# Bringing two weight matrices in transposed: by the load, in place of TensorE and ScalarE

## The chip, the cores and the metric

The kernel runs on one core of a Trainium2 chip. A core has five engines that run their own instruction streams: TensorE (PE in the profile; its weight loads are listed apart as PEld), VectorE (DVE), ScalarE (ACT), GpSimd (POOL) and SyncE (SP). Data comes from HBM and goes back to it through 16 DMA engines, which SP, ACT and POOL feed: each of the three has a queue of its own, and an issuing engine that has to wait before one transfer holds up every transfer behind it in its queue. The metric is the device time of one execution in microseconds (us). Before the change it is 1417.9 us, the median of 3 runs (1413.8 to 1419.28).

## What is computed

The kernel computes one decode step of a conditioned transformer block and its gradients. The forward, cut to what matters here:

```python
# x: [1,1,640]; k_cache, v_cache: [1,32,8192,192]; all bfloat16
q  = (h @ wq).reshape(32 heads, 192)              # h: layer norm of x, scaled and shifted by mod
p  = softmax(q @ k_cache^T * 192**-0.5)           # over 8192 positions, per head
ao = concat(p @ v_cache) @ wo                     # wo: [6144, 640]
x1 = x + ga * ao                                  # h_b: x1's layer norm, scaled and shifted
h2 = gelu(layernorm(h_b) @ w3) @ w4               # w3: [640, 1536], w4: [1536, 640]
out = x1 + gb * (h_b + h2)
```

The outputs are `out` and the gradients of x, k_cache, v_cache, wq, wo, w3, w4, c and w_mod for a given `grad_out`. (A part of the reference with w1 and w2 drops out, because with one position it only ever sees padding.) Two steps of the backward need a weight matrix with its rows and columns exchanged, since they multiply by its transpose:

- `d_n2 = du @ w3^T`, once, in the middle of the kernel;
- `do = (ga * dx1) @ wo^T`, the gradient at the attention's output, 192 numbers for each head, with rows 384t to 384t+383 of wo for the pair of heads t.

K, V and their gradients are by far the largest tensors: 201 MB of K and V are read for the forward, V is read again for the backward, and 201 MB of gradients are written.

## The kernel before, in words

The numbers that matter: D = 640 (ND = 5 blocks of 128), F = 1536 (NF = 12 blocks), 32 heads of DH = 192, 16 pairs of heads (NT; the last is TL = 15), PW = 384 rows of wo for each pair, P = 128 partitions. TensorE contracts over the partitions, so an operand's contracted index must lie along them. wo as it lies in HBM serves the forward; the backward wants it the other way round.

**Order.** The order of the instructions of TensorE, VectorE, ScalarE and SP is written out by hand (`manual_schedule`): an engine runs them in program order, and where one has to wait, all behind it on that engine wait too. Dependencies alone link the engines.

**Three stages.** First comes the forward over heads 0 to 30, half a head's K or V (1.5 MB) at a time, through five K buffers (`KB`) and three V buffers (`VB`). Then comes the middle: the last head, the MLP's forward and backward, down to `dao`, from which all of the attention's backward starts. Last comes the backward, 64 steps `s` of half a head each, heads in descending order, pair TL first. A step multiplies V with `do` (`mul_q`, VectorE), sums the products with TensorE (`tree_q`, L948) and reduces them to `dP` (L316); from these it makes dK (`dk_part`, VectorE, L964), and dV by outer products on TensorE (`dv_groups`, L959) that ScalarE copies out of PSUM (L960). POOL stores dK (L1214) and dV (L1210); SP loads V for step s+4 (L297).

**w3 in the middle.** w3 is loaded as it lies in HBM, in five row blocks (`w3v`), for the forward product `ups` (L767). For the backward, `w3t_gen` (L745 to L751) makes twelve blocks `w3Tv[a]`: five TensorE transposes of 128x128 into PSUM (L749), then one ScalarE copy (L750). The calls `w3t(n)` are spread between other work from L761 to L842. The blocks lie in two `vs` buffers (T0, T1) and in the first part of the K buffer `KC`, each free once the `m_units` that read it are through. The product with them is `dn_ps` (L850). Ahead of it on the chain: twelve VectorE products `d_g` (`dg_part`, L476), one for each row block of w4, the last of which (`load_rows(..., 11, 12)`, L617) is loaded late because its place in KC has to come free; then `du_bf` (L795).

**wo in the backward.** `load_wo(t)` (L213 to L217) brings a pair's 384 rows as [128, 3, 640] into one of two buffers with the tag `wo`; each partition gets 3840 contiguous bytes. `transposed` (L813 to L822) turns it on TensorE, 15 transposes of 128x128 (L821) with two ScalarE copies (L822), into a tile `wT`; `do_t(t, 0)` and `do_t(t, 8)` are its two parts. `do_mm(t)` (L894) multiplies with the turned tile (L901) and ScalarE scales the result into `do` (L904). The natural tile is then used a second time: `g_dwo` (L1076) overwrites it with wo's gradient, and POOL stores it from there (L1081); only then is the buffer free for another `load_wo`. For pair TL, the tile that the forward used is kept and turned, partly at L846 and partly inside the first `layernorm_bwd` (L914). Pair TL-1 is loaded at L911. The other 14 come from `g_ld`.

**The side jobs.** In the backward, work that isn't part of a step is cut into pieces, listed in `jobs` (L1141 on) and run in order by `slot()`, which is called four times a step. The first eight pieces have slots written by hand (`RAMP`); from slot R0 = 24 the others are spread evenly over the slots up to the 236th. `g_do(n)` was three pieces: `do_t`, `do_t`, `do_mm`. `g_ld`, `g_dwo` and the gradients of wq and w_mod (`g_dq`, `g_wm`, which use `transposed` too) are further jobs.

Of the kernel before, what the change touches and what calls it, by code (L numbers as in the profile page):

```python
# [20 lines left out]
def kernel(  # L21
# [186 lines left out]
    def load_w(view3, lo, hi):  # L208
        w = wst.tile([P, ND, CW], BF16, name="w_st", tag="w", bufs=1)
        nc.sync.dma_start(out=w[:, :, 0 : hi - lo], in_=view3[:, :, lo:hi])  # L210
        return w

# [116 lines left out]
    with tc.tile_pool(name="vs", bufs=3) as vsp, tc.tile_pool(name="ft", bufs=2) as ft, \  # L329
# [149 lines left out]
        with tc.manual_schedule(engines=ORDER):  # L479
# [264 lines left out]

            def w3t_gen():  # L745
                for a in range(NF):
                    tp = psR.tile([P, 1024], BF16, name="w3T_ps", tag="dot_ps")
                    for k in range(ND):
                        T_.transpose(out=tp[:, k * P : (k + 1) * P], in_=w3v[k][:, a * P : (a + 1) * P], identity=ident_bf)  # L749
                    A_.copy(out=w3Tv[a], in_=tp[:, 0:D])  # L750
                    yield  # L751

            w3t_it = w3t_gen()

            def w3t(n):
                for _ in range(n):
                    next(w3t_it, None)

            pe.pop(0)()
            pe.pop(0)()  # L760
            w3t(2)  # L761
            next(g2, None)
# [5 lines left out]
            dg_part(2)  # L768
            w3t(2)
            pe = m_units(3, ky[1], vs3, mp)  # L770
# [7 lines left out]
            V_.tensor_tensor(out=e1, in0=e1, in1=u, op=ALU.mult)  # L778
            w3t(1)
            pe.pop(0)()  # L780
            w3t(1)
            pe.pop(0)()
            pe.pop(0)()
            load_rows(flat(KC)[:, JQ * DH : JQ * DH + D], 11, 12)
            w3t(1)
            V_.tensor_scalar(out=w_, in0=w_, scalar1=1.0, scalar2=None, op0=ALU.add)
# [36 lines left out]

            woT = {}

            def do_t(t, x0):
                if x0 == 0:
                    woT[t] = w4b[:, 0 : 3 * D] if t == TL else bst.tile([P, 15 * P], BF16, name="wT", tag="wT")
                w = wo_l[t]
                transposed(x0, lambda a, b: [(0, P, w[:, a, b * P : (b + 1) * P])], 3, woT[t])  # L830

            er_ps = e_rows(TL - 1, psO, "op")
            er_ps2 = e_rows(TL, psO, "op")
            w3t(1)
            e_rows_out(TL - 1, er_ps)
            h2_mm(0, 2)
            w3t(1)
            e_rows_out(TL, er_ps2, w4b[:, F + D : F + D + P])
            h2_mm(2, 4)
            w3t(1)  # L840
            h2_mm(4, ND)
            w3t(1)  # L842
            mt = mp_out(H1 - 1, mp)
            dw4_dve(flat(KX), 0, 0, 2)
            m_add(H1 - 1, mp, mt)
            do_t(TL, 0)  # L846
            dn_ps = psS.tile([P, ND], FP32, name="dn_ps", tag="s")
# [40 lines left out]
    def do_of(h):  # L888
        return do_r[:, (TL - h // 2) % NDR, (h % 2) * DH : (h % 2 + 1) * DH]
# [20 lines left out]

    wo_l[TL - 1] = load_wo(TL - 1)  # L911
    er_l = {0: load_er(0), 1: load_er(1)}

    layernorm_bwd(d_n2, n2, r2, dbo, d_sb, "lb2", lambda: (do_t(TL, 8), dw4_dve(flat(KX), 0, 2, 4)))  # L914
    d_n1 = tcol(ND, "d_n1")
# [89 lines left out]
    def g_do(n):  # L1005
        do_t(TL - n, 0)
        yield
        do_t(TL - n, 8)
        yield
        assert done_s[0] >= 4 * (n - NDR + 1)  # L1010
        do_mm(TL - n)
        done.add(n)
        yield

    def g_ld(n):
        wo_l[TL - n] = load_wo(TL - n)
        yield
# [58 lines left out]
    def g_dwo(n):  # L1076
        t = TL - n
        w = wo_l.pop(t)
# [274 lines left out]
```

## Time and profile before

| what | us |
|---|---|
| median of 3 runs | 1417.9 |
| the profiled execution | 1418.06 |
| its span | 1416.1 |
| PE busy in it | 1190.1 (84%) |
| VectorE busy | 1108.4 (78%) |
| ScalarE busy | 893.9 (63%) |
| bytes moved by DMA | 569.35 MB, mean 402 GB/s |

The span is the time from the first to the last recorded instruction; all times below are counted from its start. The forward ends near 545 us, the middle lasts to about 583 us, and the backward fills the rest. The groups of instructions that the change concerns, as the profile gives them:

```profile
L749 PE MATMUL w3T_ps<-ident_bf,KB x22: 216/218/229, 561.7 to 570.9; 128*128 128x128 bf16 x22
L750 ACT COPY vs<-w3T_ps x8: 692/693/698, 562.2 to 568.2; 128x640 bf16<-128x640 bf16 x8
L750 ACT COPY KB<-w3T_ps x3: 692/699/712, 569.8 to 573.6; 128x640 bf16<-128x640 bf16 x3
L821 PE MATMUL wT_ps<-ident_bf,wo_st x240: 266/314/314, 573.7 to 1157.7; 128*128 128x128 bf16 x120
L822 ACT COPY wT<-wT_ps x82: 905/976/1032, 603.8 to 1347.3; 128x1024 bf16<-128x1024 bf16 x41, 128x896 bf16<-128x896 bf16 x41
```

Each line has the source line, the engine, the operation with output and inputs, the count, the shortest, median and longest duration in ns, and the first and last start in us. Of the 82 copies of L822 into `wT`, 30 belong to wo; the others belong to the gradients of wq and w_mod, which the change leaves as they are.

### The profile page before, as it was taken

How to read it: one execution, taken by the hardware profiler on the slowest of the kernel's cores; microseconds unless marked ns; L12 is line 12 of the kernel's file. 1: busy time of each engine (PE TensorE's matmuls, PEld its weight loads, DVE VectorE, ACT ScalarE, POOL GpSimd, SP SyncE). 2: the span in 40 equal slices, each digit the busy share in tenths (PEclk: the TensorE clock that was granted, in tenths of full speed). 3: DMA queues.
4: the chain of work that ended last, by engine and by line, in shares of the span. 5: the costliest groups of instructions: out<-in, count | busy, mean ns of one | idle time of the engine just before them, and what ended most of it. 6: DMA issues, size and time to landing. Idle time of an engine off the chain costs nothing.

```text
span 1416.1 us, 30395 instructions
## 1 busy us (share of the span) xinstructions
PE 1190.1 (84%) x12697; PEld 748.8 (53%) x12697; DVE 1108.4 (78%) x1418; ACT 893.9 (63%) x1952; POOL 105.3 (7%) x190
## 2 busy tenths in 40 slices
PE   3888989999999999798867997887978787779975
PEld 2777777777777777543323443443434333334431
DVE  4989999999999997886755875676766767768775
ACT  0767777777777776465645665565655565556664
POOL 0000000000000000110100110111110101111110
PEclk9999999999999999755555555565555655555555
DMA  9999999999999997599999999999999999999998
GB/s 375 394 394 416 418 415 418 411 415 414 422 415 419 411 412 274 178 391 428 424 393 420 427 423 424 420 422 422 425 420 421 411 414 410 405 400 392 424 411 355
DMA packets 76247, 569.35 MB, mean 402 GB/s; under 512 B 7342, under 2 KB 25086, under 8 KB 36046
## 3 DMA queue, kind: packets, MB, share of 16 engines
q1 hardware_dynamic: 51210, 342.02, 59.5%
q0 software_dynamic: 24368, 224.87, 38.1%
q8 instruction: 99, 1.62, 0.4%
q10 hardware_dynamic: 532, 0.53, 0.1%
q14 instruction: 38, 0.31, 0.1%
HBM read 340.95 MB, written 226.43 MB: 401 GB/s over the span
## 4 chain that ended last, share of the span: by engine, by line
issue 47%; DVE 22%; DMA 13%; PE 10%; POOL 6%; ACT 1%; SPq 0%; POOLq 0%; DVEq 0%
DVE prod L302 9%; DMA KB<-in_A_k_cache_dram 8%; DVE prod L306 5%; DVE vs L352 3%; PE mp L374 3%; DMA out_dram<-KB 3%; POOL out_dram L1214 2%; POOL out_dram L1210 2%; DMA w_st<-in_A_wq_dram 2%; PE half_ps L312 2%; PE mp L379 2%; DMA KB<-in_A_v_cache_dram 1%; DVE pq L929 1%; POOL out_dram L1054 1%; DVE KB L964 1%
## 5 line engine op out<-in xcount | busy, mean ns | idle before, releaser
L960 ACT CAST KB<-dv_ps 128x768 bf16<-128x768 f32 x512 | 397.4, 803 | 159.7 <-PE dv_ps L959 157.6
L948 PE MATMUL dot_ps<-pq,ident_bf 128*128 128x256 bf16 x1506 | 383.6, 398 | 24.0 <-DVE dP L316 22.0
L964 DVE TENSOR_TENSOR KB<-qs_bc,dS 128x3072 bf16<-128x3072 bf16 x122 | 210.7, 1753 | 129.0 <-DMA out_dram<-KB 117.0
L359 ACT ACTIVATE vs<-VB,Ef 128x192 bf16<-128x192 bf16 x840 | 303.5, 447 | 0.0
L948 PEld LDWEIGHTS <-ident_bf 128*128 128x128 bf16 x1506 | 151.9, 124 | 179.7 <-issue 140.3
L959 PE MATMUL dv_ps<-do_r,er_b 1*128 1x192 bf16 x2048 | 231.2, 338 | 4.5 <-ACT KB L960 3.2
L929 DVE TENSOR_TENSOR pq<-VB,do_r 128x3072 bf16<-128x3072 bf16 x126 | 220.4, 1749 | 15.7 <-PE dot_ps L948 15.7
L302 DVE TENSOR_TENSOR prod<-KB,qs_bc 128x6144 bf16<-128x6144 bf16 x62 | 207.9, 3353 | 26.6 <-DMA KB<-in_A_k_cache_dram 20.3
L374 PE MATMUL mp<-vs,KB 128*128 128x193 bf16 x1968 | 189.9, 249 | 3.7 <-ACT vs L359 2.6
L374 PEld LDWEIGHTS <-KB 128*128 128x128 bf16 x1984 | 171.1, 98 | 13.1 <-DMA KB<-in_A_k_cache_dram 5.3
L822 ACT COPY wT<-wT_ps 128x1024 bf16<-128x1024 bf16 x82 | 79.0, 964 | 122.6 <-PE wT_ps L821 122.2
L959 PEld LDWEIGHTS <-er_b 1*128 1x128 bf16 x2048 | 69.4, 104 | 157.5 <-issue 154.7
L312 PE MATMUL half_ps<-prod,ident_bf 128*128 128x256 bf16 x744 | 95.1, 279 | 44.4 <-DVE prod L306 44.1
L352 DVE TENSOR_TENSOR vs<-VB,E 128x1728 bf16<-128x1728 bf16 x120 | 123.7, 1052 | 0.3 <-ACT vs L359 0.3
L306 DVE TENSOR_TENSOR prod<-prod 128x3072 bf16<-128x3072 bf16 x62 | 108.7, 1754 | 1.0
L312 PEld LDWEIGHTS <-ident_bf 128*128 128x128 bf16 x744 | 72.9, 100 | 62.7 <-issue 53.6
L379 PE MATMUL mp<-vs,KB 128*64 128x193 bf16 x1968 | 105.9, 250 | 0.0
L316 DVE TENSOR_REDUCE dP<-dot_ps 128x32 f32<-128x512 f32 x64 | 44.0, 688 | 66.9 <-PE dot_ps L948 66.6
L379 PEld LDWEIGHTS <-KB 128*64 128x64 bf16 x1984 | 79.4, 109 | 20.0 <-issue 19.9
L339 ACT ACTIVATE E<-S_h,negm 128x256 bf16<-128x256 f32 x31 | 15.8, 508 | 113.9 <-DVE negm L502 111.6
L1214 POOL DMA_DIRECT2D out_dram<-KB x61 | 33.5, 549 | 475.5 <-DVE KB L964 299.8
L388 PE MATMUL op<-vs,ones_bf 128*32 128x193 bf16 x1920 | 62.1, 250 | 0.0
(300 smaller groups left out, 975.3 us busy)
## 6 DMA issues: line engine op xcount, KB each, us to landing
VB<-in_A_v_cache_dram SPq DMA_DIRECT2D x123, 1536.0 KB
out_dram<-KB POOLq DMA_DIRECT2D x123, 1536.0 KB, 16.0
KB<-in_A_k_cache_dram SPq DMA_DIRECT2D x64, 1536.0 KB
wo_st<-in_A_wo_dram SPq DMA_DIRECT2D x31, 480.0 KB
w_st<-in_A_wq_dram SPq DMA_DIRECT2D x12, 960.0 KB
out_dram<-wo_st POOLq DMA_DIRECT2D x16, 480.0 KB, 16.2
out_dram<-w_st POOLq DMA_DIRECT2D x7, 960.0 KB, 15.4
w_st<-in_w_mod_dram SPq DMA_DIRECT2D x6, 960.0 KB
```

Source lines behind the costliest of these rows:

```text
L302: V_.tensor_tensor(out=prod, in0=src, in1=vec[:, None, :].to_broadcast([P, JH, DH]), op=ALU.mult)
L306: V_.tensor_tensor(out=prod[:, :, 0:HW], in0=prod[:, :, 0:HW], in1=prod[:, :, DH - HW : DH], op=ALU.add)
L312: T_.matmul(ps, lhsT=ident_bf, rhs=prod[:, :, k : k + TF], start=(k == 0), stop=(k == w - TF))
L352: V_.tensor_tensor(out=vs[:, 0:n, 0:DH].rearrange("p j (a b) -> p j a b", b=4), in0=v[:, v0 : v0 + n, :].rearrange("p j (a b) -> p j a b", ...
L359: A_.activation(out=vs[:, k, 0:DH], in_=v[:, v0 + k, :], func=ACT.Copy, scale=Ef[:, j0 + k : j0 + k + 1])
L374: T_.matmul(mp[:, 0:MW], lhsT=kb[:, j0 + k, 0:P], rhs=vs[:, k, 0:MW], start=(q == 0 and k == 0), stop=(z and k == JQ - 1), skip_group_chec ...
L379: T_.matmul(mp[p0 : p0 + 64, MO : MO + MW], lhsT=kb[:, j0 + k, P:DH], rhs=vs[:, k, 0:MW], start=False, stop=(z and k >= JQ - 2), skip_grou ...
L929: V_.tensor_tensor(out=pq[:, q], in0=v_l[s][:, q * JQ : (q + 1) * JQ, :], in1=do_of(ht(s)[0])[:, None, :].to_broadcast([P, JQ, DH]), op=AL ...
L948: T_.matmul(ps[:, q * JQ : (q + 1) * JQ, :], lhsT=ident_bf, rhs=pq[:, q, :, k : k + TS], start=(k == 0), stop=(k == w - TS), skip_group_ch ...
L959: T_.matmul(ps[:, b, k * DH : (k + 1) * DH], lhsT=er[p0 : p0 + 1, 2 * m + k, :], rhs=doh[p0 : p0 + 1, :], start=True, stop=True)
L960: A_.copy(out=dV4[:, 2 * q : 2 * q + 2, m * PW : (m + 1) * PW], in_=ps[:, :, 0:PW])
L964: V_.tensor_tensor(out=dK[:, lo:hi, :].rearrange("p j (a b) -> p j a b", b=4), in0=qh.rearrange("p (a b) -> p a b", b=4)[:, None, :, :].to ...
```

## The change

A load may turn its data on the way: with `transpose=True`, a DMA issued by SP takes a matrix [rows, columns] and puts its columns along the partitions. The change uses that for w3 (three loads, of 512 columns each, into the places where the twelve blocks lay) and for the backward's wo (`load_woT`, one load for each pair). The layout of the turned wo differs from before: within a block of 128 columns of wo, the 384 rows now lie in their natural order, so that `do_mm` reads and writes without its rearranged views. The tile has as many bytes as before, and `g_dwo` still uses it as its output buffer. `do_t` and `w3t_gen` are gone, and `g_do` is one piece in place of three. Pair TL's wo, whose natural tile the forward has, is loaded a second time. `load_wo` stays for the forward, and `transposed` for wq and w_mod.

```diff
+    def load_woT(t):
+        w = wst.tile([P, ND * PW], BF16, name="woT", tag="wo")
+        nc.sync.dma_start(out=w.rearrange("p (i d) -> p i d", i=ND), in_=A_wo[t * PW : (t + 1) * PW, :], transpose=True)
+        return w
...
-            def w3t_gen():
-                for a in range(NF):
-                    tp = psR.tile([P, 1024], BF16, name="w3T_ps", tag="dot_ps")
-                    for k in range(ND):
-                        T_.transpose(out=tp[:, k * P : (k + 1) * P], in_=w3v[k][:, a * P : (a + 1) * P], identity=ident_bf)
-                    A_.copy(out=w3Tv[a], in_=tp[:, 0:D])
-                    yield
...
             pe.pop(0)()
             pe.pop(0)()
-            w3t(2)
+            for k, dst in enumerate((T0, T1, flat(KC))):
+                nc.sync.dma_start(out=dst[:, 0 : 4 * D].rearrange("p (a d) -> p a d", a=4), in_=B_w3[:, 4 * k * P : 4 * (k + 1) * P], transpose=True)
+            wo_l[TL] = load_woT(TL)
             next(g2, None)
...
-            def do_t(t, x0):
-                if x0 == 0:
-                    woT[t] = w4b[:, 0 : 3 * D] if t == TL else bst.tile([P, 15 * P], BF16, name="wT", tag="wT")
-                w = wo_l[t]
-                transposed(x0, lambda a, b: [(0, P, w[:, a, b * P : (b + 1) * P])], 3, woT[t])
...
     def do_mm(t, b=None):
-        wT = woT[t]
+        wT = wo_l[t]
...
         for i in range(ND):
-            rhs = wT[:, i * PW : (i + 1) * PW].rearrange("p (c a) -> p c a", c=3)[:, :, 64 * bs[0] : 64 * bs[-1] + 64]
-            T_.matmul(ps[:, 0:w], lhsT=dao_bf[:, i : i + 1].to_broadcast([P, P]), rhs=rhs, start=(i == 0), stop=(i == ND - 1))
+            lo = i * PW + DH * bs[0]
+            T_.matmul(ps[:, 0:w], lhsT=dao_bf[:, i : i + 1].to_broadcast([P, P]), rhs=wT[:, lo : lo + w], start=(i == 0), stop=(i == ND - 1))
         for k, b in enumerate(bs):
             h = 2 * t + b
-            A_.activation(
-                out=do_of(h).rearrange("p (a c) -> p a c", c=3),
-                in_=ps[:, 0:w].rearrange("p (c a) -> p a c", c=3)[:, 64 * k : 64 * k + 64, :],
-                func=ACT.Copy,
-                scale=rinv[:, h : h + 1],
-            )
-
-    wo_l[TL - 1] = load_wo(TL - 1)
+            A_.activation(out=do_of(h), in_=ps[:, k * DH : (k + 1) * DH], func=ACT.Copy, scale=rinv[:, h : h + 1])
+
+    wo_l[TL - 1] = load_woT(TL - 1)
...
     def g_do(n):
-        do_t(TL - n, 0)
-        yield
-        do_t(TL - n, 8)
-        yield
         assert done_s[0] >= 4 * (n - NDR + 1)
         do_mm(TL - n)
         done.add(n)
         yield
...
     def g_ld(n):
-        wo_l[TL - n] = load_wo(TL - n)
+        wo_l[TL - n] = load_woT(TL - n)
...
-    jobs = [(3, g_do(1)), (1 + ND // 4 + 1, g_bcast(dao, ND, dao_bc)), (1, g_dwo(0)), (1, g_ld(2)), (3, g_do(2))]
+    jobs = [(1, g_do(1)), (1 + ND // 4 + 1, g_bcast(dao, ND, dao_bc)), (1, g_dwo(0)), (1, g_ld(2)), (1, g_do(2))]
...
-            jobs.append((3, g_do(n + 3)))
+            jobs.append((1, g_do(n + 3)))
```

The pieces fall from 223 to 193, and the first eight, which `RAMP` puts on slots 5, 6, 8, 9, 10, 11, 12 and 19, are others than before. Before: `do_t`, `do_t`, `do_mm` of pair TL-1, three pieces of `g_bcast`, `g_dwo(0)`, and `g_ld(2)` on slot 19; `g_do(2)` began on slot 24. After: `g_do(1)` on slot 5, `g_bcast` on 6, 8 and 9, `g_dwo(0)` on 10, `g_ld(2)` on 11, `g_do(2)` on 12, and `g_dwo(1)` on 19.

More of the change, by code (lines that the diff above doesn't have):

```diff
@@ L743 @@
             w3Tv = [h[:, a * D : (a + 1) * D] for h in (T0, T1, flat(KC)) for a in range(4)]
-            def w3t_gen():
-                for a in range(NF):
-                    tp = psR.tile([P, 1024], BF16, name="w3T_ps", tag="dot_ps")
-                    for k in range(ND):
-                        T_.transpose(out=tp[:, k * P : (k + 1) * P], in_=w3v[k][:, a * P : (a + 1) * P], identity=ident_bf)
-                    A_.copy(out=w3Tv[a], in_=tp[:, 0:D])
-                    yield
[L753 to L757, printed above, removed]
             pe.pop(0)()
             pe.pop(0)()
-            w3t(2)
+            for k, dst in enumerate((T0, T1, flat(KC))):
+                nc.sync.dma_start(out=dst[:, 0 : 4 * D].rearrange("p (a d) -> p a d", a=4), in_=B_w3[:, 4 * k * P : 4 * (k + 1) * P], transpose=True)
+            wo_l[TL] = load_woT(TL)
             next(g2, None)
@@ L768 @@
             dg_part(2)
-            w3t(2)
             pe = m_units(3, ky[1], vs3, mp)
@@ L778 @@
             V_.tensor_tensor(out=e1, in0=e1, in1=u, op=ALU.mult)
-            w3t(1)
             pe.pop(0)()
-            w3t(1)
             pe.pop(0)()
@@ L784 @@
             load_rows(flat(KC)[:, JQ * DH : JQ * DH + D], 11, 12)
-            w3t(1)
             V_.tensor_scalar(out=w_, in0=w_, scalar1=1.0, scalar2=None, op0=ALU.add)
@@ L822, in transposed @@
                 A_.copy(out=wT[:, x0 * P : (x0 + n) * P], in_=tp[:, 0 : n * P])
-            woT = {}
-            def do_t(t, x0):
-                if x0 == 0:
-                    woT[t] = w4b[:, 0 : 3 * D] if t == TL else bst.tile([P, 15 * P], BF16, name="wT", tag="wT")
-                w = wo_l[t]
-                transposed(x0, lambda a, b: [(0, P, w[:, a, b * P : (b + 1) * P])], 3, woT[t])
             er_ps = e_rows(TL - 1, psO, "op")
             er_ps2 = e_rows(TL, psO, "op")
-            w3t(1)
             e_rows_out(TL - 1, er_ps)
             h2_mm(0, 2)
-            w3t(1)
             e_rows_out(TL, er_ps2, w4b[:, F + D : F + D + P])
             h2_mm(2, 4)
-            w3t(1)
             h2_mm(4, ND)
-            w3t(1)
             mt = mp_out(H1 - 1, mp)
@@ L845 @@
             m_add(H1 - 1, mp, mt)
-            do_t(TL, 0)
             dn_ps = psS.tile([P, ND], FP32, name="dn_ps", tag="s")
@@ L899, in do_mm @@
         for i in range(ND):
-            rhs = wT[:, i * PW : (i + 1) * PW].rearrange("p (c a) -> p c a", c=3)[:, :, 64 * bs[0] : 64 * bs[-1] + 64]
-            T_.matmul(ps[:, 0:w], lhsT=dao_bf[:, i : i + 1].to_broadcast([P, P]), rhs=rhs, start=(i == 0), stop=(i == ND - 1))
+            lo = i * PW + DH * bs[0]
+            T_.matmul(ps[:, 0:w], lhsT=dao_bf[:, i : i + 1].to_broadcast([P, P]), rhs=wT[:, lo : lo + w], start=(i == 0), stop=(i == ND - 1))
         for k, b in enumerate(bs):
             h = 2 * t + b
-            A_.activation(
-                out=do_of(h).rearrange("p (a c) -> p a c", c=3),
-                in_=ps[:, 0:w].rearrange("p (c a) -> p a c", c=3)[:, 64 * k : 64 * k + 64, :],
-                func=ACT.Copy,
-                scale=rinv[:, h : h + 1],
-            )
-    wo_l[TL - 1] = load_wo(TL - 1)
+            A_.activation(out=do_of(h), in_=ps[:, k * DH : (k + 1) * DH], func=ACT.Copy, scale=rinv[:, h : h + 1])
+    wo_l[TL - 1] = load_woT(TL - 1)
     er_l = {0: load_er(0), 1: load_er(1)}
-    layernorm_bwd(d_n2, n2, r2, dbo, d_sb, "lb2", lambda: (do_t(TL, 8), dw4_dve(flat(KX), 0, 2, 4)))
+    layernorm_bwd(d_n2, n2, r2, dbo, d_sb, "lb2", lambda: dw4_dve(flat(KX), 0, 2, 4))
     d_n1 = tcol(ND, "d_n1")
@@ L1077, in g_dwo @@
         t = TL - n
-        w = wo_l.pop(t)
+        w = wo_l.pop(t).rearrange("p (c r) -> p c r", c=3)
         for k in range(3):
```

## The prediction

> **What bounds the kernel now.** I began with the page's 40 slices and its DMA queues, then asked for the busy time of stretches, first the whole backward, then pieces of ten microseconds.
>
> ```profile
> GB/s 375 394 394 416 418 415 418 411 415 414 422 415 419 411 412 274 178 391 428 424 393 420 427 423 424 420 422 422 425 420 421 411 414 410 405 400 392 424 411 355
> q1 hardware_dynamic: 51210, 342.02, 59.5%
> q0 software_dynamic: 24368, 224.87, 38.1%
> ```
>
> Only two of the slices (35.4 us each) fall far below 400 GB/s, those around the middle stage. SP's queue (q1) and POOL's (q0) together fill 97.6% of the 16 engines' time.
>
> ```profile
> 590.00:1416.00 826.00, 677.26 (x4896) 319.47 (x4895) 581.29 (x821) 488.31 (x656) 93.60 (x164) 0.54 1.00 411
> ```
>
> Behind the stretch and its length stand the busy us of PE, PEld, DVE, ACT and POOL, then TensorE's clock, the DMA share and GB/s. Over the 826 us of the backward the DMA engines are busy at a share of 1.00; PE is busy 82%, ACT 59%. **The backward is bound by DMA**: what shortens PE or ACT there gains nothing as long as the queues stay full, and what lengthens a transfer is paid for nearly in full. How well the queues cover a stall of PE, this shows:
>
> ```profile
> PE wT_ps L821 <- DMA wo_st<-in_A_wo_dram: 20.8, 4, 12.6
> ...
> 710.00:720.00 10.00, 0.05 (x1) 0.00 (x0) 4.45 (x3) 0.13 (x1) 0.54 (x1) 0.50 1.00 421
> 720.00:730.00 10.00, 7.33 (x50) 3.89 (x50) 3.86 (x4) 5.35 (x8) 0.54 (x1) 0.50 0.95 398
> ```
>
> For pair 11 the transposes follow the load by one piece; PE stood for 12.6 us, and DMA lost 5% of the next 10 us: 0.5 us.
>
> In the middle (545 to 583 us) the DMA share is 0.38, and a chain of small operations sets the end. Its last part, from the timeline:
>
> ```profile
> 568.99 0.10 PEld L810 LDWEIGHTS <-KB 128*128 128x128 bf16 x1 [0.82 <-DMA KB<-in_B_w_dram]
> 571.96 0.82 DVE L476 CUSTOM_DVE_ANT_0 w4b<-KB,w4b 128x640 bf16<-128x640 bf16 x1
> 572.83 0.17 DVE L795 SCALAR_TENSOR_TENSOR du_bf<-t__10308,d_g 128x12 bf16<-128x12 f32 x1
> 572.99 1.29 ACT L750 COPY KB<-w3T_ps 128x640 bf16<-128x640 bf16 x2
> 574.55 0.39 PE L850 MATMUL dn_ps<-du_bf,vs 128*128 128x1 bf16 x8
> ```
>
> VectorE's twelve products set `du_bf`, ready at 573.0. `dn_ps` could start then; it starts at 574.5, because ScalarE makes the last two w3T copies only now. The last row block of w4 lands at 569.0, 3 us ahead of its product.
>
> **What is removed.** 60 transposes of w3 and 240 of wo on PE (15 of wo take 2.0 us together: 1.01 and 0.95 in the timeline), so 16 x 2.0 = 32 us for wo; 32 ScalarE copies of 0.97 us (31 us) and 12 of 0.69 us (8 us). In the backward DMA hides all of this. Gain there: only where DMA runs dry, as at 580 to 600 us (shares 0.55 and 0.80), 720 to 730 (0.95) and 1270 to 1280 (0.82). The first belongs to the start, the last has no wo transposes. Bounds 0 and -5 us; I take **-2**, by the two small gaps near wo waits (0.95 at 720, 0.97 at 620) and some of the start.
>
> **What is added in the backward.** Fourteen loads (pairs 13 to 0) become transposing; pair 14's lies in the idle middle. No transposing DMA is in this trace, so I bound its price by packets. The trace records size and time of every packet; the medians on the two queues are 460 ns for 12288 B, 149 for 3840, 65 for 1536, 18 for 256 and 9 for 4: about 8.5 ns and a byte at 27.2 per ns. Today a wo load is 128 packets of 3840 B, 128 x 149 / 16 engines = 1.19 us. To turn a matrix, the load must cut each row of 1280 B into blocks of 128 columns, 256 B: 384 x 5 = 1920 pieces x 18 ns / 16 = 2.16 us, 0.97 us more. Low end: as today, 0. High end: pieces of 64 B, 7680 x 10.9 / 16 = 5.2 us, 4.0 more. I take the 256 B row, the shape of the source's blocks: 14 x 0.97 = **+13.6** (0 to +56).
>
> [...]
>
> **What is added in the middle.** Four issues stand in SP's queue ahead of row block 11 of w4: three of w3 (640 x 4 = 2560 pieces each, 2.88 us) and pair 15's wo (2.16): 10.8 us of DMA by the same row. T0 is free when `m_units(1)` ends (558.9), T1 and KC when `m_units(2)` does (561.8). Row blocks 7 to 10 issue at 558.9 and take until about 562. So the four run from about 562 to 572.5, and row block 11, which today issues at 566.75 and lands 2.2 us later, lands near 574. Queued behind it: its product on VectorE, then `du_bf`; and on PE `h2_mm` (L810), with `dn_ps` behind that. `dn_ps` would start at about 575.5 in place of 574.5. So 1.5 us is gained from ScalarE's copies and some 2.5 lost: **+1**. If the loads take half as long, row 11 is in time and the gain of 1.4 stands; at the 64 B price (27 us) it is +17.
>
> **What moves.** In the ramp, `g_ld(2)` falls from slot 19 to 11, one slot after `g_dwo(0)`, whose store must land before the buffer is free, and `g_do(2)` follows on slot 12. Today slots 10 and 12 are at 617.6 and 621.7 us, and a wo store takes 16.2 us at the median. So SP waits from 619 to about 632 with the V load of step 7 behind it; PE stands at `do_mm` from 621.7 until wo has landed, near 636, with dV's products and, through ScalarE's scaling, the copies queued behind. The stores of steps 2 and 3 are out by about 632; then DMA is partly empty until dV comes again near 642. The same kind of stall cost 0.5 us at 710, with fuller queues; if 10 us ran dry, it costs 10. I take **+4** (0.5 to 10). Later, `g_ld` to `g_do` is six pieces at 185/212 = 0.87 a slot, 6.9 slots of 3.25 us = 22 us (before: 19 to the first transpose); a wo load lands 16.2 us after its issue at the median (9.3 to 25.0), so cover is left.
>
> **The sum**, against the profiled execution (1418.06 us, its span 1416.1 and 2 around it; the median of the runs, 1417.9, is the same within 0.2): -2 + 13.6 + 1 + 4 = +16.6. **Forecast: 1434 us.** Its own range is 1421 (a packet price of a third, no ramp stall) to 1446 (the ramp at its worst, 0.4 us more a load).
>
> **Rivals.**
>
> *Turned loads cost no more than plain ones* (on the other side: faster). The place is the backward's DMA. Then the terms are 0 for the packets, -1.4 in the middle, 0 to +0.5 in the ramp and up to -5 for PE and ACT: **1412**. It decides as long as a load costs under 6.4 / 14 = 0.46 us more than today. For it: the bytes are the same, and PE's clock of 0.54 leaves its stretches little slack around 800 to 900 us (87% busy). Against it: a DMA share of 1.00 that leaves nothing to gain, and a 256 B packet that moves 14 B per ns where one of 3840 B moves 26.
> [...]
>
> *The small pieces lose their turns.* The queues take turns packet by packet: w_st loads of 1536 B (40 packets per engine) ran from first to last packet in 4.4 to 6 us in the forward, but in 17 to 22 us in the backward among POOL's 12288 B packets. A turned wo load has 120 pieces per engine. At 18 + 460 ns a turn it would last 57 us, unless POOL runs dry first: five K buffers of 1.5 MB at 424 GB/s hold 18 us. Then wo lands near 32 us, `do_mm` is 10 us late for each pair, and V loads behind it on SP come late too. At 0.5 to 3 us of dry DMA a pair, this adds 7 to 42 to the forecast: **1460**. For it: the 17 to 22 us. Against it: DMA goes on working while pieces wait, and the wait at 710 cost 0.5 us.
>
> *The load is slow in itself*, holding the engines for several times its bytes. At 64 B pieces the terms are +56, +17, +4, -2: **1493**. Nothing in the trace speaks for pieces that small, and nothing excludes it.
> [...]
>
> *The change doesn't do what it says*: moved as single elements, a load is 245,760 x 8.6 ns / 16 = 132 us; 3000 us and more. 1 in 100.
>
> **How the numbers follow.** The forecast (1421 to 1446) has 0.44; the faster rival (1408 to 1421) 0.24; lost turns (1446 to 1485) 0.20; slow in itself 0.11; single elements 0.01. The range is 1411 to 1480: about 0.07 lies below and 0.13 above. A difference of 0.5% (7 us) is about what a measurement of this kernel can tell from no change. Faster by more, under 1411, is the better part of the first rival, since it needs every gain or a covered gap that I did not see: 0.15. Within it, to 1425: the rest of that rival and the low edge of the forecast: 0.17. Slower: 0.68.
>
> **What would show it.** Packets: the wo loads as about 1920 pieces of 256 B and near 18 ns, and a DMA share of the backward still at 1.00. The middle: `dn_ps` starting within 2 us of today's distance from `ups`, with no ScalarE copy ahead. The ramp: one long PE wait at L901 for a wo load near 622 us, and a DMA share under 0.9 in the 20 us behind it. No copies of wo in L822's group (52 left). Wrong I am if the share falls well under 1.00 (then waits decide, and turns or holds on SP are the cause), if the pieces take much more or less than 18 ns, or if the backward is shorter at equal GB/s.

## The result and the profile after

The changed kernel takes **1653.5 us** (median of 4 runs, 1640.0 to 1677.4). The kernel before took 1416.4 beside it (4 runs, 1413.8 to 1419.3). The ratio is **1.164, 95% interval 1.156 to 1.173**: 237 us more, where +16.6 was forecast. Single runs of the kernel before lie between 1412 and 1423 us in the comparisons below. One of the four runs (1677.4) was in the slower state, as were the highest of e7 and of e10: the medians here and below count these runs, the ratios leave them out. The profiled execution has a span of 1655.9 us.

First the page's slices (41.4 us each) and its two data queues:

```profile
GB/s 382 394 419 413 412 416 412 418 418 410 421 415 412 226 285 330 414 236 311 406 386 286 285 291 207 215 221 368 233 349 221 222 230 367 425 402 410 412 392 339
q1 hardware_dynamic: 88058, 344.48, 64.4%
q0 software_dynamic: 24368, 224.87, 36.1%
```

Before, two slices fell far below 400 GB/s. Of the 21 slices from the middle on (the 14th to the 34th), now only two are above 400, and fifteen are under 340, down to 207. From the 35th, behind 1407 us, the rate is back above 400 until the last two. The bytes are nearly as before: q1 has 2.5 MB more, w3 a second time (1.97) and pair 15's wo (0.49). Its 36,848 more packets come from the pieces of the turned loads.

Next stretches of the backward: behind the stretch and its length stand the busy us of PE, PEld, DVE, ACT and POOL, then TensorE's clock, the DMA share and GB/s.

```profile
590.00:1650.00 1060.00, 650.65 (x4688) 295.46 (x4684) 583.45 (x824) 464.63 (x627) 93.51 (x164) 0.53 1.03 319
...
900.00:1000.00 100.00, 47.09 (x342) 21.39 (x339) 43.57 (x63) 33.70 (x45) 6.95 (x12) 0.50 1.09 262
1000.00:1100.00 100.00, 38.98 (x291) 17.84 (x290) 36.33 (x57) 28.77 (x40) 6.26 (x11) 0.55 1.18 191
1400.00:1500.00 100.00, 81.17 (x603) 38.56 (x603) 69.04 (x120) 55.76 (x73) 9.30 (x16) 0.50 1.01 411
```

The first line answers to the 826 us of before. Two columns must be read together here. The share says that the DMA engines are fully busy (1.03, and 1.09 and 1.18 in the two stretches inside), but they move 319, 262 and 191 GB/s, against 411 before and in the last line. So they are not short of work; their packets last longer. PE, VectorE and ScalarE are about half as busy as in the last line, whose stretch lies behind the last turned load (it ends at 1355 us). The backward is bound by DMA as before, and DMA has slowed down.

What the turned loads of wo do shows in the list for the tile `woT` (shortest, median and longest duration in ns of SP's instruction, first and last start in us; then issue to landing):

```profile
L216 SPq DMA_TRANSPOSE woT<-in_A_wo_dram x16: 1730/35761/49207, 569.5 to 1298.5; - x16
...
DMA to landing us min/median/max: 6.1/15.5/49.8
```

and in SP's timeline, for one of them:

```profile
867.89 37.40 SPq L216 DMA_TRANSPOSE woT<-in_A_wo_dram  x1
905.39 1.99 SPq L303 DMA_DIRECT2D VB<-in_A_v_cache_dram  x2
```

One instruction keeps SP for 1.7 us in the middle, for 36 us at the median, and the V loads queue behind it (here until 905 us). The waits (engine, what for, whom for: total us, times, longest) show where this arrives, first in the changed kernel, then, for the same stores, in the one before:

```profile
DVE KB L936 <- DMA out_dram<-KB: 211.7, 32, 36.8
...
PE do_ps L878 <- DMA woT<-in_A_wo_dram: 141.2, 7, 26.9
```

```profile
DVE KB L964 <- DMA out_dram<-KB: 117.0, 32, 8.4
```

VectorE waits for POOL's stores to leave the K buffers, which the change doesn't touch: the stores have become slow as well. The longest of these waits has grown from 8.4 to 36.8 us. In the packet records, 166 store packets (141 of 12288 B, 25 of 7680 B) lasted over 2 us, where in the kernel before none did (for 12288 B 1.2 us at the most, 460 ns at the median).

The trace records start, duration, queue and size of every packet. A turned load of wo has 1920 pieces of 256 B, with a median of 18 ns, just as the prediction had it; but the mean over all turned pieces, w3's included, is 90 ns, one in twenty lasts 474 ns or more, and the longest 18.5 us. A turned load that met stores only at its two ends (841.6 to 843.9 us) took 2.3 us, all its pieces 18 ns. Nine others, beside stores, took 31 to 49 us from first to last piece. I call **lost time** what a stretch of pieces (no more than 1.5 us apart) lasts beyond all the bytes that moved in it at 420 GB/s, about the rate that the backward otherwise has (422 from 1000 to 1100 us in the kernel before). Over the 14 loads of the backward it comes to 199 us.

### The profile page after: what moved, and what is told of

Read it like the earlier page. It is cut to its first block, busy times and chain, and to the rows that moved or that the text cites. A ratio compares the mean times of both kernels' runs of the same rounds, so it can differ in the third digit from the quotient of the medians.

```text
span 1655.9 us, 29790 instructions
## 1 busy us (share of the span) xinstructions
PE 1159.1 (70%) x12402; PEld 720.5 (44%) x12402; DVE 1109.1 (67%) x1418; ACT 860.8 (52%) x1909; POOL 105.2 (6%) x190
## 3 DMA queue, kind: packets, MB, share of 16 engines
q0 software_dynamic: 24368, 224.87, 36.1%
## 4 chain that ended last, share of the span: by engine, by line
issue 45%; DMA 19%; DVE 18%; PE 9%; POOL 4%; another core or an unknown queue 3%; ACT 1%; SPq 1%; POOLq 0%; DVEq 0%
DMA KB<-in_A_k_cache_dram 8%; DVE prod L308 8%; DMA out_dram<-KB 6%; DVE prod L312 4%; DMA woT<-in_A_wo_dram 3%; PE mp L380 3%; DVE vs L358 2%; PE half_ps L318 2%; POOL out_dram L1182 2%; POOL out_dram L1178 2%; PE mp L385 2%; DMA w_st<-in_A_wq_dram 1%; DVE KB L936 1%; PE dot_ps L920 1%
## 5 line engine op out<-in xcount | busy, mean ns | idle before, releaser
L380 PEld LDWEIGHTS <-KB 128*128 128x128 bf16 x1984 | 171.1, 98 | 13.6 <-DMA KB<-in_A_k_cache_dram 5.9
L878 PE MATMUL do_ps<-woT,dao_bf 128*128 128x384 bf16 (+1 forms) x85 | 27.8, 490 | 142.6 <-DMA woT<-in_A_wo_dram 141.2
L881 ACT ACTIVATE do_r<-do_ps,rinv 128x192 bf16<-128x192 f32 x32 | 11.8, 418 | 167.8 <-PE do_ps L878 167.8
L812 ACT COPY wT<-wT_ps 128x1024 bf16<-128x1024 bf16 (+1 forms) x52 | 50.0, 962 | 67.6 <-PE wT_ps L811 67.5
L878 PEld LDWEIGHTS <-dao_bf 128*128 128x128 bf16 x85 | 11.5, 138 | 153.4 <-issue 150.7
```

The costliest lines, as they stand in the source:

```text
L380: T_.matmul(mp[:, 0:MW], lhsT=kb[:, j0 + k, 0:P], rhs=vs[:, k, 0:MW], start=(q == 0 and k == 0), stop=(z and k == JQ - 1), skip_group_chec ...
```

## The experiments

The theory after the result: the time is lost where turned pieces and POOL's stores are under way together, because a turned load goes through the 16 DMA engines in step, and an engine that holds a turned piece does nothing else until the others come up. Rivals: the small pieces alone do it; the long SP hold does it (V loads come late); the loads are slow in themselves; the ramp and the middle.

### e1: the loads by themselves and beside stores

The whole computation is left out. Stages follow one another: eight stores of 1.5 MB by POOL, alone and beside three wo loads by SP, which are plain, in 256-byte pieces, or turned.

```diff
+    for load in (None, plain, pieces, turned):
+        for st in (None, 0, 1):          # no stores, 12288-byte packets, small packets
...
+            if st is not None:
+                stores(st)
+            for k in range(3):
+                if load is not None:
+                    load(k, (t := (t + 1) % NT))
+            fence()
```

> This kernel leaves the whole computation out: it only moves data, in stages parted by VectorE writes that wait for all transfers of the stage. A stage is 8 stores of 1.5 MB by POOL (none, with packets of 12288 B, or with packets of 1536 B) beside 3 wo loads of 480 KB by SP (none, plain with 3840 B per partition, cut into pieces of 256 B without turning, or turned by the load). Lockstep theory: a turned load moves in steps that need all 16 engines at once, and at each step some engine is busy with a store packet, while the others wait idle. Alone the three turned loads take about 3 x 2.3 = 7 us and some 2 more to land; beside 12288 B stores, at the 190 GB/s that the bursts after the change show, the stage's 14 MB take 74 us, against 36 us for the sum of both alone; beside 1536 B stores, whose packets last 65 ns and not 460, 45 us at the most; the 256 B pieces that are not turned cost no more than their packets (stage 36 us). Lost turns alone (the pieces wait, but DMA goes on working): turned and unturned pieces behave alike, and every stage lasts as long as its packet times together, 34 to 41 us, whatever the store packets.

Stretches of this run, which was taken once: stores alone, plain loads with stores, pieces with stores, turned loads alone, turned loads with stores (busy columns only for DVE and POOL):

```profile
70.90:107.00 36.10, 5.89 (x43) 4.37 (x8) 1.00 0.84 349
157.30:196.00 38.70, 5.91 (x43) 4.23 (x8) 1.00 0.87 363
...
252.65:289.20 36.55, 5.96 (x44) 4.27 (x9) 1.00 0.89 358
331.10:342.40 11.30, 5.59 (x41) 0.03 (x1) 1.00 0.73 131
342.40:391.70 49.30, 5.89 (x44) 4.21 (x8) 1.00 0.98 285
```

The three turned loads alone took 7.1 us of their stage from first to last piece: 2.4 us each, so they aren't slow in themselves (three plain ones took 5.1). Turned loads beside the stores: 49.3, which is 6 us more than stores and turned loads one after the other (36.1 + 7.1), and 10.6 more than plain loads of the same bytes beside the same stores (38.7). The direction is that of the theory, the size isn't: it had put 74 us, and the rival without any loss 34 to 41.

The stage of the pieces can't be set against these. What ends a stage touches the first 16 columns of each tile, and of the three transfers of a load in pieces only the first writes there. SP ran ahead with the other two, and only 1920 of the 5760 pieces fell among the stores (36.5 us). What unturned pieces cost is left to e2.

Most packets of the stores with smaller packets were 4608 B long and not 1536, so that the turned loads' stage beside them (49.7 us against 41.6 for the stores alone, where 45 at the most was expected) tells less of the packet's length than it was meant to. In a last stage the turned loads stand between V loads of 1.5 MB in SP's own queue, without stores. Its packets take 20.0 us from first to last, against 12.3 for the V loads alone: 7.7 more, about what the turned loads take by themselves. So plain loads ahead of a turned one in the same queue cost next to nothing here.

### e2: the same pieces, not turned

```diff
-        nc.sync.dma_start(out=..., in_=A_wo[t * PW : (t + 1) * PW, :], transpose=True)
+        for c in range(3):
+            nc.sync.dma_start(out=w.rearrange("p (i c d) -> p i c d", i=ND, c=3)[:, :, c, :],
+                in_=A_wo[t * PW + c * P : t * PW + (c + 1) * P, :].rearrange("p (i d) -> p i d", i=ND))
```

> The kernel after, with the backward's wo loads cut into pieces of 256 B but not turned, so that do and what follows from it come from an untransposed matrix; w3 is still turned. Lockstep theory: the small pieces alone are paid by their packet times, so the time is near the 1434 us that I had forecast, 1420 to 1445. Lost turns (small pieces on SP's queue beside large store packets, late wo and late V): most of the 237 us stays, above 1550 us. Hold of SP by the turning instruction: gone with it, since a plain load doesn't hold SP, so also near 1434; the store packets then show whether DMA was ever slow.

1453.3 us (1451.3 to 1454.5), ratio 1.025 (1.023 to 1.028), 8 us above the range expected. With the same 1920 pieces in the same places of SP's queue, 200 of the 237 us are gone. The same stretch as above, and SP's instructions for these loads, three to a load:

```profile
900.00:1000.00 100.00, 74.54 (x591) 34.10 (x589) 73.50 (x112) 55.83 (x77) 11.79 (x20) 0.62 1.02 414
```

```profile
L217 SPq DMA_DIRECT2D woT<-in_A_wo_dram x48: 545/1302/22509, 567.3 to 1143.2; - x48
```

Beside the stores the pieces last up to 34 us from first to last here too. But of the nine loads that lasted over 16 us, eight have 392 to 416 GB/s passing meanwhile. Lost time over all loads: 12 us, and no store packet over 2 us. So here small pieces that waited their turn cost the others next to nothing (12 us), and turned ones 199. That a plain load doesn't hold SP, as was expected, is not so for small pieces: over the 14 loads they keep SP for 226 us. The turned loads keep it for 444.

### e3 and e5: plain loads, and the ramp's slots

e3 loads wo as the kernel before did, but doesn't transpose it; e5 does the same with `RAMP` so that `g_ld(2)` is again on slot 19.

```diff
-        nc.sync.dma_start(out=..., in_=A_wo[t * PW : (t + 1) * PW, :], transpose=True)
+        nc.sync.dma_start(out=w.rearrange("p (c r) -> p c r", c=3), in_=wo_v[t])
...
-    RAMP = {5: 1, 6: 1, 8: 1, 9: 1, 10: 1, 11: 1, 12: 1, 19: 1}
+    RAMP = {8: 1, 9: 1, 10: 1, 11: 1, 12: 1, 19: 1}
```

> The kernel after, with the backward's wo loads as before (3840 B a partition, not turned, so do is computed from an untransposed matrix); no transposes of wo on TensorE, no copies on ScalarE, w3 turned, and the ramp as after. It shows what the change would be worth if turning wo cost nothing. All theories: the remaining terms of the prediction, -2 for PE and ACT, +1 in the middle, +4 in the ramp: about 1421 us (1412 to 1428). If PE and ACT were what held the backward, it falls below 1405.

> As e3 (the backward's wo loaded untransposed, 3840 B a partition, so do comes from an untransposed matrix), with the eight early side jobs put back where they were in time: do_mm of pair 14 on slot 8, bcast on 9 to 11, g_dwo(0) on 12, g_ld(2) on 19, g_do(2) from slot 24. If e3's +13 us is the ramp's stall (its DMA share was 0.82 from 620 to 660 us, against 1.00 before), the time falls to 1416 to 1421 us. If it is the sparser spread of the later pieces or the middle, it stays above 1427. If PE's and ScalarE's removed work was worth anything in the backward, it falls below e4's 1414.7.

e3: 1430.8 us (1424.6 to 1440.2), ratio 1.0095 (1.0066 to 1.0124), a little above the range expected. e5: 1420.0 (1416.4 to 1425.1), ratio 1.0022 (1.0006 to 1.0037), in its range. Three sums follow. The ramp costs 1430.8 - 1420.0 = 10.8 us. The pieces cost 1453.3 - 1430.8 = 22.5. And without any transpose or copy of wo on PE and ScalarE, with the old ramp, the kernel is 2.5 us longer than the one before (1417.5 beside it): what PE and ScalarE were relieved of bought nothing that shows. It is even 5.3 us longer than e4 below, which still turns wo on TensorE; why isn't shown. The ramp's stretch, of e3 and then of e5:

```profile
620.00:660.00 40.00, 19.84 (x155) 8.79 (x154) 21.70 (x19) 15.66 (x22) 3.15 (x6) 0.67 0.82 329
```

```profile
620.00:660.00 40.00, 34.29 (x204) 13.19 (x202) 25.89 (x23) 23.15 (x31) 3.72 (x7) 0.50 1.01 426
```

(426 - 329) GB/s x 40 us is 3.9 MB, or 9 us of DMA: nearly the whole difference is in these 40 us.

### e4 and e9: only w3 turned by the load

e4 is the kernel before with the three turned loads of w3. In e9 the third of them stands behind row block 11 of w4 instead of ahead of it.

```diff
-            for k, dst in enumerate((T0, T1, flat(KC))):
-                nc.sync.dma_start(out=..., in_=B_w3[:, 4 * k * P : 4 * (k + 1) * P], transpose=True)
+            w3_turned(0, T0)
+            w3_turned(1, T1)
...
             load_rows(flat(KC)[:, JQ * DH : JQ * DH + D], 11, 12)
+            w3_turned(2, flat(KC))
```

> Only the w3 part of the change: w3 turned by three loads in the middle, wo as before on TensorE and ScalarE, the ramp as before. Lockstep theory and lost turns alike: in the middle nothing is stored, so the three loads take 3 us each, and row block 11 of w4 lands near 573: +1 to +2 us, 1418 us, within 0.3% of before. If the turned load is slow whatever lies beside it (16 us for 480 KB, so 21 us each for w3), 1470 us.

> Only w3 is turned by the load, as in e4_w3_only, but the third turned load (into KC) now stands behind row block 11 of w4 in SP's queue instead of ahead of it. Theory (in the middle a turned load costs only the place it takes in SP's queue: in e4 VectorE's last product waited 1.50 us and PE's h2_mm 5.89 for row block 11): that wait is gone, VectorE's twelve products run without a gap, and the time is 1 to 2 us under e4: 1412.5 to 1414, 0.2 to 0.35% under the kernel before. Rival (the order of SP's queue is not what sets the middle, the third turned load is needed just as late): the wait moves from row block 11 to dn_ps, which waits for KC, and the time is e4's 1414.7 within 1 us.

e4: 1414.7 us (1413.1 to 1417.9), ratio 0.9985 (0.9972 to 0.9997). e9: 1414.5 (1410.7 to 1416.6), ratio 0.9974 (0.995 to 0.9998). VectorE's last product in e4, and `dn_ps` in e9:

```profile
570.52 0.83 DVE L476 CUSTOM_DVE_ANT_0 w4b<-KB,w4b 128x640 bf16<-128x640 bf16 x1 [1.50 <-DMA KB<-in_B_w_dram]
```

```profile
570.05 0.17 DVE L782 SCALAR_TENSOR_TENSOR du_bf<-t__10282,d_g 128x12 bf16<-128x12 f32 x1
...
574.14 0.27 PE L833 MATMUL dn_ps<-du_bf,KB 128*128 128x1 bf16 x4 [2.87 <-DMA KB<-in_B_w_dram]
```

With row block 11 ahead, VectorE's products run without a gap, and `du_bf` is ready at 570.05. But now PE waits for KC: the third turned load lands near 574.1, 7.9 us after its issue at 566.27. The wait only moved, as the rival had it, and e9 can't be told from e4. Both are a little under the kernel before, by 0.02 to 0.5%; they are the only versions that are. Where e4's 2.5 us come from isn't shown: in its profile the chain through the middle is 1.2 us longer than before.

### e6 and e10: stores held while a turned load is under way

GpSimd reads a corner of the landed tile, so that the stores that POOL issues later wait for it. Stores already in the queue go on (2 to 32 of their packets start in a microsecond around one such load of e10, in its table below). e10 has e5's ramp as well.

```diff
         wo_l[TL - n] = load_woT(TL - n)
+        gate = tmp.tile([P, 16], BF16, name="gate")
+        nc.gpsimd.tensor_copy(out=gate, in_=wo_l[TL - n][:, 0:16])
```

> The kernel after, with one small GpSimd copy after each of the 14 turned loads, which reads the landed tile: POOL's later stores are issued only when wo has landed. Nothing is left out. Lockstep theory (a turned load is slow only beside store packets): the bursts of pieces shorten from 17 to 48 us to under 10 where the stores queued before have drained, packets of 12288 B over 2 us become rare, and the time falls well under 1653, to about 1530 (1450 to 1600), the rest being stores held back. If the turned load is slow by itself in this kernel, the stores' wait comes on top: 1700 us or more.

> e6_stores_held (GpSimd's later stores wait while a turned wo load is under way), with the ramp's slots of the kernel before, so that pair 13's wo load is again issued at slot 19. Theory (the ramp costs 10.8 us on its own, as e3 against e5 showed with plain loads, and the cost of the turning is another sum): 1462 - 11 = 1451 us, ratio near 1.025, and the PE wait for woT near 622 us is gone. Rival (in the ramp there is no steady stream of stores, so the turned loads or the gates hide or replace this stall): within 4 us of 1462. What is left over 1420 after this is then the smaller pieces (about 22 us by e2 against e3) and the gates.

e6: **1462.1 us** (1453.6 to 1473.4), ratio 1.032 (1.028 to 1.037), near the low end of its range. Of the 237 us, 191 are gone, though the loads are turned as in the changed kernel and POOL stands at the gates for 240 us:

```profile
POOL gate L986 <- DMA woT<-in_A_wo_dram: 240.1, 14, 24.2
```

```profile
900.00:1000.00 100.00, 79.37 (x555) 35.17 (x554) 69.48 (x109) 54.77 (x75) 18.59 (x22) 0.53 1.04 400
```

The loads now last 2.4 to 15 us, one of them 22, the lost time is 26 us, and 17 store packets last over 2 us. That settles that a turned load is dear by the stores beside it, and not by itself. The long hold of SP has gone with them: SP stands in the turned loads for 229 us in place of 444. That is as long as in e2 (226), and the two kernels are within 9 us of each other; a hold of 444 us without slow packets was not tried.

e10: 1498.3 us (1488.3 to 1544.8), ratio 1.054 (1.050 to 1.059). Both expectations missed: it is 36 us slower than e6, not 11 faster. The stall in the ramp is gone, as it was in e5; the loss has come back elsewhere:

```profile
620.00:660.00 40.00, 31.74 (x189) 12.43 (x188) 31.06 (x30) 21.15 (x29) 5.52 (x10) 0.50 1.03 407
...
800.00:900.00 100.00, 57.51 (x403) 26.01 (x402) 47.96 (x76) 41.43 (x56) 11.09 (x16) 0.53 1.05 306
```

(e6 has 295 and 401 GB/s in these.) With the same gates, the loads fall at other moments, and the lost time is 82 us in place of 26. This run shows best what goes on in such a load. Counted from the packet records, for each microsecond from the given time: packets started by POOL's stores, turned pieces started, other packets over 512 B started, and pieces that were held all through it.

```
e10       stores  pieces  others  held pieces
772 us      32       0      34         0
775          2       0     245         0
776          2     432     112         0
778          2       0       2        21
782          2       0       2        21
786          2       0       2        21
788          2      24       0         0
791         15     888       0         0
```

At 772 the stores start 32 packets of 460 ns in a microsecond, two for each of the 16 engines, and between them go 1536-byte packets of the load ahead of wo. At 776 nearly all are through and start on the turned load. But one engine still has stores in its queue and 1536-byte packets in SP's, and takes them in turn: from 777 to 788 the records hold a single chain of 460, 65, 460, 65 ns. For these 11 us the pieces that the others have begun stand (21 of them, for 10.9 to 12.2 us), and the engines with them, until that one engine gets to its own first turned piece. The records name no engine; that the chain is one engine's is read from its packets, which follow one another without overlap. The whole stretch from 776 to 792 us loses 13 us.

In the changed kernel, a load that cost nearly nothing and one that cost 21 us look like this:

```
after     stores  pieces  others  held over 1 us
770 us      34      35       1      none
776         34      36       0      none
782         25     104       0      none

904          9      51       0      none
908         11      44       1      none
916          2      33       0      none
922          2       3       0      15 of 12288 B
```

At 770 the stores' 34 packets in a microsecond are work for all 16 engines (34 x 460 ns = 15.6 us), and one piece goes with each: 392 GB/s, 1.1 us lost. From 904 on only 2 to 11 store packets start in a microsecond, the work of a few engines. The reading that fits: each step of the turned load waits for one of their packets, and the other engines wait along. At 922 the held packets are 11 of the stores and 4 of a V load. By these cases it isn't stores as such that make a turned load dear, but that some engines have more of them left than the others. No run varies that alone.

### e7 and e8: shorter store packets

dK and dV are stored in four parts, which makes packets of 3072 B out of 12288: e7 in the changed kernel, e8 in the one before.

```diff
-        nc.gpsimd.dma_start(out=dK_hd[h][:, t * JH + lo : t * JH + hi, :], in_=dK[:, lo:hi, :])
+        for j in range(lo, hi, 8):
+            nc.gpsimd.dma_start(out=dK_hd[h][:, t * JH + j : t * JH + j + 8, :], in_=dK[:, j : j + 8, :])
```

> The kernel after, with the dK and dV stores cut into four (8 positions each, packets of 3072 B), nothing left out. Lockstep theory: the step of a turned load is one store packet, so it falls from 470 to about 130 ns, the bursts to under 20 us, and the loss of 200 us to a third: about 1530 us (1480 to 1580), less what e8 shows the cut to cost. If the loss is a hold that doesn't depend on the packets' length (the engines' queues, SP's hold), it stays near 1653.

> The kernel before with the same cut stores, for e7's comparison. A packet of 3072 B takes 121 ns where a quarter of one of 12288 B takes 115: 5% of the 475 us that 201 MB of stores take, +24 us, and POOL issues 4 x 123 transfers at 0.53 us, 260 us in all, hidden: about 1440 us (1420 to 1460), by all theories.

e7: 1578.6 us (1563.2 to 1588.6), ratio 1.111 (1.106 to 1.115), at the upper end of its range. e8: 1442.1 (1441.2 to 1444.5), ratio 1.018 (1.017 to 1.019). With short packets the change costs 1578.6 - 1442.1 = 136 us in place of 237. The direction is as expected, the size isn't: a third was expected, 58% is left. By the reading above, a shorter packet makes each step shorter (in the kernel before, packets of 3072 B took 121 ns at the median, those of 12288 B 460) but leaves an engine that is behind just as many bytes behind. That this is the reason has not been tried by itself.

### The lost time against the times

| kernel | time, us | lost time in the wo loads, us |
|---|---|---|
| e2, pieces not turned | 1453.3 | 12 |
| e6, turned, stores held | 1462.1 | 26 |
| e10, the same, other ramp | 1498.3 | 82 |
| e7, turned, short packets | 1578.6 | 109 |
| changed kernel | 1653.5 | 199 |

From e2 to the changed kernel the lost time grows by 187 us and the time by 200. From e2 to e7 it is 97, beside 125 in time, of which the short packets account for 25 (e8). From e6 to e10 it is 56, beside 36 in time, where the ramp should have given 11 back. The one measure accounts for nearly all of what turning costs. It says where the time went; that the stores are the cause rests on e2 and e6.

## Why the prediction was wrong

Taking the steps in its order:

- **What bounds the kernel: right.** DMA set the backward, and a slower transfer was paid for nearly in full: from e2 to the changed kernel 187 us more of lost time, 200 us more of time.
- **What is removed (-2): nothing shows.** e5 has none of wo's transposes and copies and is 2.5 us over the kernel before. In the changed kernel, L812's group has 52 copies, as the prediction said.
- **What is added in the backward (+13.6): the step that failed**, with "1920 pieces x 18 ns / 16 = 2.16 us, 0.97 us more". The number of pieces, their size and their median were right, and a load that had the engines nearly for itself took 2.3 us. But the 18 ns are those of the 20 packets of 256 B in the kernel before, none of them turned, and dividing by 16 takes the engines to be independent of each other. The packet records of e10, with 21 pieces held for 10.9 to 12.2 us beside a single chain, speak against that. In place of +13.6 the runs showed 22.5 us for the pieces (e2 against e3) and some 200 us for the turning beside stores (changed kernel against e2; e6). The upper end of this term, +56, priced smaller pieces, that is the same mistake with another number.
- **The rival "the small pieces lose their turns" had the place and dismissed the price.** It had the 460 ns store packets between the pieces, wo landing late and V loads late behind it on SP, at 1460. Its argument against, "DMA goes on working while pieces wait", is true of plain pieces: in e2 they last as long and lose 12 us. For turned pieces it is false, and with it the 0.5 to 3 us a pair become 199 / 14 = 14.
  The 460, 65, 460, 65 ns of e10 agree with queues that take turns packet by packet.
- **The rivals "Turned loads cost no more than plain ones" and "The load is slow in itself" fall alike.** Alone, three turned loads of 491,520 B take 7.1 us (e1), about 207 GB/s: slower than plain ones (5.1 us), and 2.4 us each, under half of the 5.2 us that 64 B pieces were put at.
- **The middle (+1): right in its mechanism, a little too small.** Row block 11's product waited for its load, until 574.9 us where 574 was forecast, in the changed kernel's VectorE timeline:

```profile
574.94 0.82 DVE L482 CUSTOM_DVE_ANT_0 w4b<-KB,w4b 128x640 bf16<-128x640 bf16 x1 [3.79 <-DMA KB<-in_B_w_dram]
```

  `dn_ps` followed at 576.2. From the attention's last output to the first product of the backward, the changed kernel's profile has 31.8 us, 2.9 more than before, where the term had 1. w3 alone (e4) came out 2.5 us ahead.
- **The ramp (+4): right in its mechanism, too small.** It measured 10.8 us, just above the upper end of 10. PE's one long wait came where it was put, and ended at 639.5 in place of 636:

```profile
639.51 1.76 PE L878 MATMUL do_ps<-woT,dao_bf 128*128 128x384 bf16 x5 [22.64 <-DMA woT<-in_A_wo_dram]
```

  DMA's share in these 40 us fell to 0.87 in the changed kernel and 0.82 in e3. The sum took 4 by the stall at 710 us, which had full queues behind it; here they ran dry, which is what its upper end had priced.
- **What would show it wrong** named "if the pieces take much more or less than 18 ns", which is what happened (a mean of 90, at a median of 18), and "if the share falls well under 1.00", which did not: the share rose to 1.03 over the backward while the rate fell to 319 GB/s.

The parts together: 10.8 (ramp) + 22.5 (pieces) + 200 (turning beside stores) + 2.5 (e5 over the kernel before) = 236 us. As each is a difference of two medians along one row of kernels, they had to add up; what is shown is the size of each.

**What stays open** is why an engine falls behind the others by 10 us and more. The records don't say which of the 16 engines sent a packet, so that the steps themselves are a reading of the packets' times. It is open too why the lost time in e10 is three times that in e6, beyond the loads falling at other moments.

## What to carry to other kernels

A price from packets of independent engines didn't hold for a transfer that seems to use all of them in step: before a turned load goes into a stage whose DMA is full, measure it beside that stage's stores, not alone. It is cheap where the queues are quiet (2.4 us each alone in e1, and no loss for w3 in the middle: 1414.7 us in e4), and where it must go beside stores, hold the stores meanwhile, which brought 1653 down to 1462 us (still 3% over the kernel before), or leave the turning to an engine that has time. And read the DMA share with the GB/s beside it: a held packet counts as busy (a share of 1.18 at 191 GB/s in the changed kernel from 1000 to 1100 us).

## What the runs showed of the hardware that was not expected

- A turned load seems to hold the DMA engines in step: in e10 a single chain of packets, 11 us long, went on while 21 pieces stood for 10.9 to 12.2 us each, and nothing else moved.
- The hold reaches past the load: in the changed kernel up to 15 store packets at a time stood with it, some for over 7 us, against 460 ns at the median.
- SP stays in the instruction of a turned load through much of its pieces' way (867.9 to 905.3 us for one whose pieces ran from 877.5 to 926): 1.7 us at the least, 49.2 at the most. A plain wo load kept it for 0.3 to 1.2 us in e3, but one in 256-byte pieces for up to 28 us in e2 (its three instructions together), so that the long hold goes with the small pieces and not with the turning alone.
- Plain 256-byte pieces wait just as long for their turns (up to 34 us from first to last in e2), yet lose hardly anything: 12 us over all loads, with 392 to 416 GB/s passing meanwhile in eight of the nine longest.
